# Solve steps uncut and split otherwise over the slots, two decays moved into the first solve's slots, a longer pause ahead of a solve, some conversion steps on VectorE, nine weight loads issued sooner

## The chip, the cores and the metric

The kernel runs on one core of a Trainium2 chip. The metric is the device time of one execution in microseconds (us), lower is better. The engines are TensorE (PE; its weight loads are listed apart as PEld), VectorE (DVE), ScalarE (ACT), GpSimd (POOL) and SyncE (SP), which issues the DMA transfers.

## What is computed

Three stages follow one another. The first is a recurrence over 768 time steps for 4 x 8 heads of width 40, the second a gated layer of three weight matrices over 3072 tokens, the third a layer with a softmax-weighted activation and a normalisation.

```python
for t in range(S):                       # S = 768
    y[:, :, t] = einsum('bhd,bhde->bhe', r_t, state)
    Sa = einsum('bhde,bhe->bhd', state, a_t)
    state = state * w_t[..., None, :] - einsum('bhd,bhe->bhde', Sa, b_t) + einsum('bhd,bhe->bhde', v_t, k_t)
x = y.transpose(0, 2, 1, 3).reshape(3072, 320)
x = (sigmoid(x @ w_gate) * (x @ w_val)) @ w_out          # 320 -> 1536 -> 320
h = x @ w_in                                             # 320 -> 1024
e = exp(h - max(h)); u = h * e / (sum(e) + 1e-9)
out = ((u - mean(u)) / sqrt(var(u) + 1e-6) * g_ln) @ w_out2
```

## The kernel before

**Recurrence.** Time is cut into 24 chunks of 32 steps, and the 32 heads into two sets, which gives 48 slots s = 0 to 47. Two chunks form a superstep. Inside a chunk the state's update is a triangular system, so for each of the 12 supersteps a 32 x 32 unit-triangular matrix per head and chunk is inverted on VectorE. This is a solve, n = 0 to 11. A solve has 31 steps j (`t_iter`, L247 to L263), and a step is a multiplication into `tmp` (L258) and an addition into `pT` (L262), both over m = j//2+1 column groups of k = 31-j elements. In the solves n = 0 and n = 2 the steps from j = 6 on are `cut`: each of the two operations is made in two halves, so a step has four instructions. A solve reads its coefficients from the tile `M`, which is loaded back from DRAM (`t_load`, `M<-ab`), after TensorE's products were stored there (`ab<-abn`). Its result goes through ACT into `TT` (L268), to DRAM, and back as `TB`.

**Lookahead and slots.** The preparation of chunk data runs LOOK = 10 slots ahead, so slots are counted from s = -10; `begin` does the first four of them as a prologue and the loop over `slot` starts at s = -6. Solve 0 takes slots -6 to -3, eight steps in each. Solve n > 0 takes the four slots s = 4n-5 to 4n-2; `SOLVE` (L34) says at which steps it is split among them (k = 0 to 3), with one entry for n = 1, one for n = 2 and one for all n from 3 on. A decay (`decay`, L145 to L162, five VectorE instructions) turns a superstep's weights `G` into the factors that scale the chunk data. A decay is named by superstep and head set. `begin` does those of superstep 0, then (1,0), (1,1) and (2,0), the last three behind the first load of `M`.

**How a slot orders its work.** A slot has ten pieces of TensorE work (state products, the update, `pY` at L387 and others). VectorE's solve steps, decays and a pause form the list `back` of (cost, function). After each piece, entries are taken from `back` until their costs reach the sum that is left divided by the pieces that are left. The pause is an entry of cost WAIT with no function, ahead of a solve's first step. Only the order in which instructions stand in an engine's stream depends on this.

```python
share, left = [], sum(x for x, _ in back) / (len(work) - p)
while back and (left > 0 or p == len(work) - 1):
    x, f = back.pop(0)
    share.append(f)
    left -= x
fill(s, share)
```

**Layers beside it.** `Between.fill` (L940 to L968) mixes in the second stage: up to s = 5 the conversion of its weights, later its matrix products for the tokens that are done. The weights come as 64-bit floats and are converted by `Convert.value` (L594 to L610) into 32-bit ones: two ACT operations (L591, L592), four on VectorE (L603 to L608) and two on `self.eng` (L609, L610), which is POOL. A matrix product in 32-bit accuracy is made from high and low parts (`mm320`, L823), which ACT (L539) and POOL or VectorE (L540) split off. Behind the slots, from about 680 us to 945 us, `Late.first` (L1065) makes the remaining tokens' second stage; its `jobs2` convert the third stage's weights `w_in` and `w_out2` in the three places `l_cv`, each filled by a load of three DMAs (L624, and L529 twice). `Late.second` is the third stage.

**Queues.** All DMAs are issued by SP in the program's order; an engine takes its own instructions in the order in which they stand.

Of the kernel before, what the change touches and what calls it, by code (L numbers as in the profile page):

```python
# [17 lines left out]
ALU = mybir.AluOpType  # L18
# [6 lines left out]
CH = 32  # L25
# [5 lines left out]
KEEP = LOOK + 2  # L31
TS = SS * CH
WCOLS = TS + 2
SOLVE = (0, 0, 13, 26, 31), (0, 0, 11, 21, 31), (0, 12, 24, 28, 31)  # L34
WAIT = 2.0
LOAD = 6
SUMS = 6, 8
NF = 5
# [18 lines left out]
def run(gen, n=None):  # L57

    if gen is not None:
        for f in itertools.islice(gen, n):  # L60
            f()
# [6 lines left out]
class Attention:  # L68
# [178 lines left out]
    def t_iter(self, n, j):  # L247

        nc = self.nc
        M, TT = self.M[n], self.pT.rearrange("p (j t) -> p j t", t=CH)  # L250
        k, m = CH - 1 - j, j // 2 + 1
        tmp = self.tmp[j % 2][:, 0:m * k].rearrange("p (c t) -> p c t", t=k)

        cut = m // 2 if m >= 4 and n in (0, 2) else 0
        parts = [r for r in (slice(0, cut), slice(cut, m)) if r.stop > r.start]

        def mult(r):
            nc.vector.tensor_tensor(out=tmp[:, r], in0=TT[:, r, j:j + 1].broadcast_to([128, r.stop - r.start, k]),  # L258
                                    in1=M[:, j:j + 1, j + 1:CH].broadcast_to([128, r.stop - r.start, k]), op=ALU.mult)

        def add(r):
            nc.vector.tensor_tensor(out=TT[:, r, j + 1:CH], in0=TT[:, r, j + 1:CH], in1=tmp[:, r], op=ALU.add)  # L262
        return [(0.155 + (r.stop - r.start) * k * 0.00104, lambda r=r, f=f: f(r)) for f in (mult, add) for r in parts]  # L263

    def t_store(self, n):
        self.M.pop(n)
# [140 lines left out]
    def begin(self, dummy):  # L407

        self.w_load(1, 0)
        for i in (0, 1):  # L410
            self.clear(i)
        for i in (0, 1):
            self.w_sums(0, i)
        dummy(BEGIN[0])
        for i in (0, 1):
            for f in self.decay(0, i):
                f()
            self.scaled(i)
            if i == 0:
                self.scaled(2)  # L420
                self.w_load(1, 1)
                self.le_load(2 * SS)
                self.w_sums(1, 0)
        self.scaled(3)
        self.le_load(2 * SS + 1)
        self.w_load(2, 0)
        for k, i in enumerate((0, 2, 1, 3)):
            if k == 2:
                self.eye()
            run(self.products(i))  # L430
            dummy(BEGIN[1 + k])
        self.t_load(0)
        self.w_sums(1, 1)
        for n, hs in ((1, 0), (1, 1), (2, 0)):
            for f in self.decay(n, hs):
                f()

    def slot(self, s, fill):
        pi = s + LOOK
        pj = pi - 1  # L440
        on, last = 0 <= s < NHS, 1 <= s <= NHS

        back = []

        n, k = divmod(s - (2 * SS + 1 - LOOK), 2 * SS)
        if 0 < n < NSS:
            if k == 0:
                back += [(WAIT, None)]
            steps = range(*SOLVE[min(n, 3) - 1][k:k + 2])
            back += [f for j in steps for f in self.t_iter(n, j)]  # L450
            if k == 2 * SS - 1:
                back += [(0.0, lambda: self.t_store(n))]
        if s in range(-6, -2):
            back += [f for j in range((s + 6) * 8, min((s + 7) * 8, CH - 1)) for f in self.t_iter(0, j)]
        m, hs = pi // (2 * SS) + 1, (pi % (2 * SS)) // 2
        if pi % 2 and (2, 0) < (m, hs) < (NSS, 0):
            self.w_load(m, hs)
        if pi + 1 < NHS:
            if pi > 2 * SS:
                self.le_load(pi + 1)  # L460
            m, hs = divmod(pi + 1, 2 * SS)
            if hs < 2 and (m, hs) > (2, 0):
                back += zip((0.5, 1.3, 0.4, 1.3), self.decay(m, hs))
        late = s == -1
        if pi < NHS and not late:
            self.scaled(pi)
        ruv = self.m_ruv(s - 1) if last else None
        prod = self.products(pj) if 2 * SS <= pj < NHS else None
        work = [
            lambda: on and (run(self.m_r(s)), self.m_st(s)),  # L470
            lambda: run(ruv, 4),
            lambda: run(ruv),
            lambda: on and self.m_u(s),
            lambda: run(prod, 4),
            lambda: (run(prod), late and self.scaled(pi)),
            lambda: last and run(self.m_y(s - 1)),
            lambda: on and self.m_state(s),
            lambda: (on and self.m_ut(s), 0 <= s + 1 < NHS and self.natural(s + 1), self.loads(s + 2)),
            lambda: None]
        for p, f in enumerate(work):  # L480
            f()
            if p == LOAD and pj % (2 * SS) == 2 * SS - 1 and 2 * SS < pj < NHS:
                self.t_load(pj // (2 * SS))
            if p == 4 and s % 2 and 3 < s < NHS - 1:
                self.t_fetch((s + 1) // 2)
            if p == SUMS[pi % 2]:
                m, hs = divmod(pi + 2, 2 * SS)
                if hs < 2 and (2, 0) < (m, hs) < (NSS, 0):
                    self.w_sums(m, hs)
# [7 lines that stand above are left out]
        if s == -3:  # L497
            self.t_store(0)
            self.t_fetch(0)
        if s in (1, 3):  # L500
            self.t_fetch((s + 1) // 2)
# [213 lines left out]
def mix(take, n, other):  # L715

    other = list(other)
    for i in range(n):
        for f in [take()] + [other.pop(0) for _ in range(-(-len(other) // (n - i)))]:
            if f is not None:  # L720
                f()
    for f in other:
        if f is not None:
            f()
# [24 lines left out]
class Conversions:  # L749
# [47 lines left out]
    def next(self):  # L797

        if not self.todo and not self.over():
            self.todo = self.begin()  # L800
        return self.todo.pop(0) if self.todo else None
# [64 lines left out]
class Between:  # L866
# [68 lines left out]
    def dummy(self, k):  # L935
        z = self.zero
        for _ in range(k):
            self.nc.tensor.matmul(self.gv, lhsT=z[:, 0:128], rhs=z, start=True, stop=True)

    def fill(self, s, other, flat):  # L940

        p = self.seen[s] = self.seen.get(s, -1) + 1
        if s < FILL:
            if s >= -1:
                self.dummy(2 if s >= 0 or p > 3 else 0)
            if s == -5 and p < 3:
                self.jobs.load()
            self.cv.eng = self.nc.gpsimd
            mix(self.jobs.next, STEPS[s] if s >= 0 else 2 if s == -1 and p < 7 else 0, other)
            if s == FILL - 1:  # L950
                if p == FIRST[0]:
                    self.jobs.to(99)
                    self.begin(flat.memory)
                    self.load(0)
                if p == FIRST[1]:
                    self.ready(0)
            return
        b, k = divmod(s - FILL, 4)
        if p in LAST.get(s - NHS, UNITS) and not self.step(b):
            self.dummy(IDLE)  # L960
        mix(self.jobs2.next if not self.jobs2.over() or self.jobs2.todo else lambda: next(flat.run, None), LATER[self.jobs2.over()][p], other)
        if k == 3 and b + 1 < NT // 256:
            if p == NEXT[0]:
                if b == 1:
                    self.jobs2.to(99)
                self.load(b + 1)
            if p == NEXT[1]:
                self.ready(b + 1)  # L968
# [15 lines left out]
class Late:  # L984
# [80 lines left out]
    def first(self, btw):  # L1065
        nc, acc, hid = self.nc, [x[:, 0:D] for x in (self.lt[:, 0], self.lt[:, 1], self.one, self.three)], self.hid
        nc.sync.dma_start(out=self.gain, in_=self.d["moe2_g_ln"].rearrange("(k p) -> p k", p=128))
        tiles = [range(N0 if b == 0 else NF, 12) for b in range(6)]
        units = [(b, f) for b in range(6) for f in tiles[b]]

# [440 lines left out]
```

## Time and profile before

| | us |
|---|---|
| median of 3 runs | 1159.73 (1158.47 to 1161.88) |
| profiled execution: its time | 1161.03 |
| profiled execution: its span | 1159.3 |
| PE busy | 1030.9 (89%) |
| DVE busy | 792.8 (68%) |
| ACT busy | 594.5 (51%) |
| POOL busy | 466.7 (40%) |
| PE's mean granted clock | 0.947 of full speed |

The profile page divides the span into 40 slices of 29 us. VectorE is at 8 to 9 tenths in the first seven slices and at 7 to 9 up to the seventeenth; PE starts at 4 to 8 tenths and is at 8 or 9 from the tenth slice on. Slot 0 begins at about 65 us, slot 47 at about 643 us, `Late.first` at about 680 us and `Late.second` at about 945 us.

### The profile page before, as it was taken

To read this page: it belongs to the slowest core of one execution; us is meant where nothing else is said; L and a number is where in the kernel's file an instruction comes from. 1 tells how busy PE (TensorE), PEld (TensorE's weight loads), DVE (VectorE), ACT (ScalarE), POOL (GpSimd) and SP (SyncE) were. 2 spreads that over 40 slices of the span, in tenths; PEclk is the share of its full clock that TensorE was granted. 3 is DMA by queue.
4 is the path that set the end of the run, shared out by engine and by line. 5 is a ranking of instruction groups with operands and counts; after the bars stand their busy time and mean duration, and the time that the engine had idled before them with its cause. 6 is when DMAs were issued, how large, how long until landed. Compare 5 with 4: busy or idle time off the path is not lost.

```text
span 1159.3 us, 31815 instructions
## 1 busy us (share of the span) xinstructions
PE 1030.9 (89%) x12710; PEld 879.1 (76%) x12710; DVE 792.8 (68%) x2085; ACT 594.5 (51%) x1511; POOL 466.7 (40%) x489
## 2 busy tenths in 40 slices
PE   4287788898999998999999989799999998999997
PEld 2244457777787887888888888688888876888897
DVE  9869899888978879788683235334443369767673
ACT  5245455766666566675666444324343344444542
POOL 7564534446556456464221112234433301322232
PEclk8578998999999999999999989899999999999999
DMA  7564564668666776666534234302211000000001
GB/s 183 140 149 116 140 154 114 143 180 197 169 155 158 192 189 156 156 161 167 129 111 126 68 110 125 105 28 89 85 57 34 1 1 6 19 23 18 18 23 38
DMA packets 179451, 122.62 MB, mean 106 GB/s; under 512 B 106016, under 2 KB 159264, under 8 KB 179296
## 3 DMA queue, kind: packets, MB, share of 16 engines
q1 hardware_dynamic: 179296, 120.52, 40.1%
q8 instruction: 102, 1.67, 0.6%
q14 instruction: 53, 0.43, 0.1%
HBM read 98.94 MB, written 21.53 MB: 104 GB/s over the span
## 4 chain that ended last, share of the span: by engine, by line
PE 50%; DVE 23%; DMA 10%; ACT 7%; issue 4%; SPq 4%; POOL 1%; DVEq 0%; ACTq 0%; POOLq 0%
PE hid L823 20%; DVE pT L262 5%; DVE tmp L258 4%; PE one L823 4%; DMA b_plain<-xT 3%; PE three L1194 2%; DMA M<-ab 2%; PE three L1197 2%; PE three L1195 2%; PE pY L387 2%; DVE RL L374 2%; PE pruv L370 2%; PE two L1181 2%; PE two L856 2%; PE two L858 2%
## 5 line engine op out<-in xcount | busy, mean ns | idle before, releaser
L823 PE MATMUL hid<-l_x,l_w 128*128 128x512 f32 x672 | 161.3, 392 | 0.0
L823 PEld LDWEIGHTS hid<-l_x,l_w 128*128 128x128 f32 x672 | 125.2, 189 | 24.4 <-issue 0.2
L823 PE MATMUL one<-b_tokens,b_w 128*128 128x256 f32 x816 | 128.8, 302 | 2.1 <-DVE b_plain L844 1.7
L258 DVE TENSOR_TENSOR tmp<-pT,M 128x30 f32<-128x30 f32 (+34 forms) x422 | 96.8, 239 | 41.7 <-DMA M<-ab 32.8
L224 POOL TENSOR_TENSOR AT<-abn,mA 64x256 f32<-64x256 f32 x96 | 81.8, 852 | 82.1 <-ACT abn L219 77.2
L823 PEld LDWEIGHTS one<-b_tokens,b_w 128*128 128x128 f32 x816 | 107.7, 197 | 7.8 <-DVE b_plain L844 1.9
L262 DVE TENSOR_TENSOR pT<-pT,tmp 128x30 f32<-128x30 f32 (+34 forms) x422 | 105.2, 249 | 12.3
L540 POOL TENSOR_TENSOR l_x<-l_plain,l_x 128x512 fp32r<-128x512 f32 x43 | 55.6, 1292 | 119.6 <-ACT l_x L539 100.5
L540 POOL TENSOR_TENSOR b_tokens<-b_plain,b_tokens 128x256 fp32r<-128x256 f32 x58 | 47.6, 820 | 125.4 <-ACT b_tokens L539 113.0
L823 PE MATMUL hid<-b_w,l_x 128*128 128x512 f32 x384 | 94.0, 397 | 2.6 <-DVE l_e L1153 2.6
L844 DVE TENSOR_TENSOR l_plain<-hid,l_plain 128x512 f32<-128x512 f32 x43 | 29.7, 691 | 95.1 <-ACT l_plain L843 95.1
L207 PE MATMUL pABK<-AT,BK 128*64 128x64 f32 x768 | 62.4, 239 | 34.9 <-POOL BK L197 33.9
L207 PEld LDWEIGHTS pABK<-AT,BK 128*64 128x64 f32 x768 | 54.5, 150 | 45.7 <-POOL BK L197 36.2
L823 PEld LDWEIGHTS hid<-b_w,l_x 128*128 128x128 f32 x384 | 70.9, 188 | 19.0 <-DVE l_e L1153 3.6
L196 POOL TENSOR_TENSOR AT<-AT,G 40x256 f32<-40x256 f32 x90 | 69.0, 766 | 33.4 <-DVE G L162 19.3
L387 PE MATMUL pY<-RL,YR 128*64 128x32 f32 (+1 forms) x1536 | 59.8, 220 | 24.8 <-DVE RL L374 21.8
L387 PEld LDWEIGHTS pY<-RL,YR 128*40 128x40 f32 (+1 forms) x1536 | 52.1, 131 | 37.3 <-DVE RL L374 22.0
L843 ACT ACTIVATE l_plain<-hid 128x512 f32<-128x512 f32 x43 | 25.6, 595 | 95.2 <-PE hid L823 95.2
L314 ACT ACTIVATE Z<-pu 32x160 f32<-32x160 f32 x192 | 56.2, 293 | 28.6 <-PE pu L311 25.5
L539 ACT ACTIVATE b_tokens<-b_plain 128x256 fp32r<-128x256 f32 (+1 forms) x70 | 33.9, 488 | 63.6 <-DVE b_plain L844 45.5
L370 PE MATMUL pruv<-RL,UV 128*64 128x64 f32 x768 | 58.9, 232 | 6.4 <-ACT YR L237 2.7
L1188 POOL TENSOR_TENSOR l_w<-l_e,l_w 128x1024 fp32r<-128x1024 f32 x12 | 28.8, 2400 | 88.7 <-ACT l_e L1149 51.1
(253 smaller groups left out, 2593.2 us busy)
## 6 DMA issues: line engine op xcount, KB each, us to landing
AT<-in_LA_dram SPq DMA_DIRECT2D x48, 256.0 KB
RL<-in_RS_dram SPq DMA_DIRECT2D x24, 512.0 KB
LB<-in_LB_dram SPq DMA_DIRECT2D x46, 208.0 KB
Z<-in_VN_dram SPq DMA_DIRECT2D x48, 160.0 KB
M<-ab SPq DMA_DIRECT2D x24, 256.0 KB
UV<-in_VT_dram SPq DMA_DIRECT2D x24, 208.0 KB
G<-in_LW_dram SPq DMA_DIRECT2D x22, 214.5 KB
xT<-yt SPq DMA_DIRECT2D x24, 160.0 KB
```

What stands on the lines that cost most here:

```text
L196: eng.tensor_tensor(out=at[SROW[g], g], in0=at[SROW[g], g], in1=G[SROW[g]], op=ALU.mult)
L207: yield lambda m=m: nc.tensor.matmul(ps[0:64, m * 64:m * 64 + 64], lhsT=bkt[:, m].rearrange("p s t -> p (s t)"), rhs=at[:, :, m, :], start ...
L224: nc.gpsimd.tensor_tensor(out=at[UROW[g], g].rearrange("p (a b) t -> p a b t", a=2), in0=abn[UROW[g], :, hs], in1=self.mA[UROW[g]].unsquee ...
L258: nc.vector.tensor_tensor(out=tmp[:, r], in0=TT[:, r, j:j + 1].broadcast_to([128, r.stop - r.start, k]), in1=M[:, j:j + 1, j + 1:CH].broad ...
L262: nc.vector.tensor_tensor(out=TT[:, r, j + 1:CH], in0=TT[:, r, j + 1:CH], in1=tmp[:, r], op=ALU.add)
L314: nc.scalar.activation(z[32 * q:32 * q + 32, hs, g, p * 4:p * 4 + 4, :], ps[32 * q:32 * q + 32, 0:160].rearrange("p (h d) -> p h d", d=40) ...
L370: yield lambda p=p, hh=hh, m=m: nc.tensor.matmul(ps[0:64, m * 64:m * 64 + 64], lhsT=uvt[:, hs * 4 + hh, 64 * p:64 * p + 64], rhs=rl[:, hs, ...
L387: yield lambda m=m, g=g, at=at: nc.tensor.matmul(ps[rows[g], m * CH:m * CH + CH], lhsT=flat[:, at:at + rows[g].stop - rows[g].start], rhs= ...
L539: nc.scalar.activation(h, src, AF.Copy)
L540: eng_l.tensor_tensor(out=l, in0=src, in1=h.bitcast(F32), op=ALU.subtract)
L823: nc.tensor.matmul(out, lhsT=a, rhs=b, start=n == 0, stop=n == 7)
L844: self.nc.vector.tensor_tensor(out=self.sg, in0=self.pv, in1=self.sg, op=ALU.mult)
```

## The change

SOLVE's entry for n from 3 on goes from 12, 12, 4 and 3 steps in the four slots to 9, 12, 6 and 4. WAIT goes from 2 to 4. No step is cut any more. The decays (1,1) and (2,0) leave `begin` and come into the slots -6 and -3. L609 and L610 go to VectorE while s < 3. `Late.first` issues the loads of all three `l_cv` places right behind the load of the gain.

```diff
@@ -31,8 +31,8 @@
 KEEP = LOOK + 2
 TS = SS * CH
 WCOLS = TS + 2
-SOLVE = (0, 0, 13, 26, 31), (0, 0, 11, 21, 31), (0, 12, 24, 28, 31)
-WAIT = 2.0
+SOLVE = (0, 0, 13, 26, 31), (0, 0, 11, 21, 31), (0, 9, 21, 27, 31)
+WAIT = 4.0
 LOAD = 6
 SUMS = 6, 8
 NF = 5
@@ -251,16 +251,12 @@
         k, m = CH - 1 - j, j // 2 + 1
         tmp = self.tmp[j % 2][:, 0:m * k].rearrange("p (c t) -> p c t", t=k)
 
-        cut = m // 2 if m >= 4 and n in (0, 2) else 0
-        parts = [r for r in (slice(0, cut), slice(cut, m)) if r.stop > r.start]
-
-        def mult(r):
-            nc.vector.tensor_tensor(out=tmp[:, r], in0=TT[:, r, j:j + 1].broadcast_to([128, r.stop - r.start, k]),
-                                    in1=M[:, j:j + 1, j + 1:CH].broadcast_to([128, r.stop - r.start, k]), op=ALU.mult)
-
-        def add(r):
-            nc.vector.tensor_tensor(out=TT[:, r, j + 1:CH], in0=TT[:, r, j + 1:CH], in1=tmp[:, r], op=ALU.add)
-        return [(0.155 + (r.stop - r.start) * k * 0.00104, lambda r=r, f=f: f(r)) for f in (mult, add) for r in parts]
+        def mult():
+            nc.vector.tensor_tensor(out=tmp, in0=TT[:, 0:m, j:j + 1].broadcast_to([128, m, k]), in1=M[:, j:j + 1, j + 1:CH].broadcast_to([128, m, k]), op=ALU.mult)
+
+        def add():
+            nc.vector.tensor_tensor(out=TT[:, 0:m, j + 1:CH], in0=TT[:, 0:m, j + 1:CH], in1=tmp, op=ALU.add)
+        return [(0.155 + m * k * 0.00104, f) for f in (mult, add)]
 
     def t_store(self, n):
         self.M.pop(n)
@@ -431,9 +427,8 @@
             dummy(BEGIN[1 + k])
         self.t_load(0)
         self.w_sums(1, 1)
-        for n, hs in ((1, 0), (1, 1), (2, 0)):
-            for f in self.decay(n, hs):
-                f()
+        for f in self.decay(1, 0):
+            f()
 
     def slot(self, s, fill):
         pi = s + LOOK
@@ -459,7 +454,7 @@
             if pi > 2 * SS:
                 self.le_load(pi + 1)
             m, hs = divmod(pi + 1, 2 * SS)
-            if hs < 2 and (m, hs) > (2, 0):
+            if hs < 2 and (m, hs) > (1, 0):
                 back += zip((0.5, 1.3, 0.4, 1.3), self.decay(m, hs))
         late = s == -1
         if pi < NHS and not late:
@@ -945,7 +940,7 @@
                 self.dummy(2 if s >= 0 or p > 3 else 0)
             if s == -5 and p < 3:
                 self.jobs.load()
-            self.cv.eng = self.nc.gpsimd
+            self.cv.eng = self.nc.vector if s < 3 else self.nc.gpsimd
             mix(self.jobs.next, STEPS[s] if s >= 0 else 2 if s == -1 and p < 7 else 0, other)
             if s == FILL - 1:
                 if p == FIRST[0]:
@@ -1065,6 +1060,8 @@
     def first(self, btw):
         nc, acc, hid = self.nc, [x[:, 0:D] for x in (self.lt[:, 0], self.lt[:, 1], self.one, self.three)], self.hid
         nc.sync.dma_start(out=self.gain, in_=self.d["moe2_g_ln"].rearrange("(k p) -> p k", p=128))
+        for _ in self.jobs2.cv.raw:
+            self.jobs2.load()
         tiles = [range(N0 if b == 0 else NF, 12) for b in range(6)]
         units = [(b, f) for b in range(6) for f in tiles[b]]
```

VectorE's order at the end of the prologue, before: the two decays `G1_1` and `G2_0`, then step 0 of solve 0 (`M0`).

```order
L145 TENSOR_SCALAR G1_1_270<-G1_1_270 104x8x64
L155 SCALAR_TENSOR_TENSOR Q0_189<-G1_1_270,d1_150 104x528
L159 RECIPROCAL d1_150<-Q0_189 104x8
L160 COPY PE1_1_376<-Q0_189 104x8
L162 SCALAR_TENSOR_TENSOR G1_1_270<-G1_1_270,d1_150 104x528
L145 TENSOR_SCALAR G2_0_292<-G2_0_292 104x8x64
L155 SCALAR_TENSOR_TENSOR Q1_190<-G2_0_292,d1_150 104x528
L159 RECIPROCAL d1_150<-Q1_190 104x8
L160 COPY PE2_0_382<-Q1_190 104x8
L162 SCALAR_TENSOR_TENSOR G2_0_292<-G2_0_292,d1_150 104x528
L258 TENSOR_TENSOR tmp0_187<-pT_185,M0_365 128x31
L262 TENSOR_TENSOR pT_185<-pT_185,tmp0_187 128x31
```

VectorE's order with the change, at the end of solve 0's first eight steps (lines of the functions behind `t_iter` are three to five lower).

```order
L255 TENSOR_TENSOR tmp0_187<-pT_185,M0_365 128x100
L258 TENSOR_TENSOR pT_185<-pT_185,tmp0_187 128x4x25
L255 TENSOR_TENSOR tmp1_188<-pT_185,M0_365 128x96
L258 TENSOR_TENSOR pT_185<-pT_185,tmp1_188 128x4x24
L145 TENSOR_SCALAR G1_1_270<-G1_1_270 104x8x64
L155 SCALAR_TENSOR_TENSOR Q0_189<-G1_1_270,d1_150 104x528
L159 RECIPROCAL d1_150<-Q0_189 104x8
L160 COPY PE1_1_376<-Q0_189 104x8
L162 SCALAR_TENSOR_TENSOR G1_1_270<-G1_1_270,d1_150 104x528
L255 TENSOR_TENSOR tmp0_187<-pT_185,M0_365 128x115
L258 TENSOR_TENSOR pT_185<-pT_185,tmp0_187 128x5x23
```

Decay (1,1) now stands inside solve 0, between its eighth and ninth step; decay (2,0) stands behind solve 0's last step, ahead of decay (2,1).

VectorE's order at the first steps of solve 6 (`M6`) before; RL is the mask over the state's read rows that `pY` needs, `b_plain` a split of the second stage.

```order
L608 TENSOR_SCALAR flat_135<-flat_135 128x224
L258 TENSOR_TENSOR tmp0_187<-pT_185,M6_4730 128x31
L262 TENSOR_TENSOR pT_185<-pT_185,tmp0_187 128x31
L258 TENSOR_TENSOR tmp1_188<-pT_185,M6_4730 128x30
L262 TENSOR_TENSOR pT_185<-pT_185,tmp1_188 128x30
L374 TENSOR_TENSOR RL1_182<-pruv18_4841,mR_148 64x256 x2
L844 TENSOR_TENSOR b_plain_126<-one_123,b_plain_126 128x256
```

The same place with the change.

```order
L603 TENSOR_SCALAR flat_135<-flat_135 128x224
L255 TENSOR_TENSOR tmp0_187<-pT_185,M6_4630 128x31
L258 TENSOR_TENSOR pT_185<-pT_185,tmp0_187 128x31
L255 TENSOR_TENSOR tmp1_188<-pT_185,M6_4630 128x30
L370 TENSOR_TENSOR RL1_182<-pruv18_4741,mR_148 64x256 x2
L839 TENSOR_TENSOR b_plain_126<-one_123,b_plain_126 128x256
L258 TENSOR_TENSOR pT_185<-pT_185,tmp1_188 128x30
```

Three solve instructions instead of four stand ahead of RL; the first step stands where it stood.

SP's order at the start of `Late.first`, before.

```order
L656 DMA l_plain<-late_moe_w_out 128x320
L1067 DMA b_plain<-in_moe_g_ln_dram 128x8x1
L925 DMA x2d_116<-b_plain 128x2x320
L862 DMA l_plain<-xT_66 128x2x256
L529 DMA l_plain<-xT_66 64x256 x2
```

The same place with the change.

```order
L651 DMA l_plain<-late_moe_w_out 128x320
L1062 DMA b_plain<-in_moe_g_ln_dram 128x8x1
L619 DMA l_cv<-in_moe_w_in_dram 128x2x256
L524 DMA l_cv<-in_moe_w_in_dram 64x256 x2
L619 DMA l_cv<-in_moe_w_in_dram 128x2x256
L524 DMA l_cv<-in_moe_w_in_dram 64x256 x2
L619 DMA l_cv<-in_moe_w_in_dram 128x2x256
L524 DMA l_cv<-in_moe_w_in_dram 64x256 x2
L920 DMA x2d_116<-b_plain 128x2x320
```

The nine DMAs, which stood behind the loads for the second block of tokens, now stand ahead of the store of the last `x2d` block and of all that follows.

## Rows read from the trace of the kernel before

**Rows 1.** The page's chain that ended last: shares of the span by engine.

```profile
PE 50%; DVE 23%; DMA 10%; ACT 7%; issue 4%; SPq 4%; POOL 1%; DVEq 0%; ACTq 0%; POOLq 0%
```

**Rows 2.** Windows: stretch, length, busy us (PE, PEld, DVE, ACT, POOL), clock, DMA share, GB/s.

```profile
65.00:132.00 67.00, 49.57 (x718) 28.85 (x705) 50.28 (x133) 36.37 (x106) 36.32 (x40) 0.90 0.65 158
132.00:196.00 64.00, 51.25 (x848) 37.26 (x850) 59.88 (x199) 32.19 (x96) 29.46 (x36) 0.87 0.51 127
```

**Rows 3.** VectorE's timeline, prologue and solve 0: start, duration, instruction, [idle before <-releaser].

```profile
21.35 0.68 DVE L145 TENSOR_SCALAR G<-G 104x512 f32<-104x512 f32 x1
...
29.57 0.19 DVE L258 TENSOR_TENSOR tmp<-pT,M 128x31 f32<-128x31 f32 x1
...
38.89 0.35 DVE L258 TENSOR_TENSOR tmp<-pT,M 128x54 f32<-128x54 f32 x2
...
39.81 0.36 DVE L258 TENSOR_TENSOR tmp<-pT,M 128x68 f32<-128x68 f32 x2
```

**Rows 4.** ACT's timeline: `TT` copy behind solve 0, a gate weight, the late `l_cv`.

```profile
54.31 0.60 ACT L268 ACTIVATE TT<-pT 128x512 f32<-128x512 f32 x1 [10.48 <-DVE pT L262]
...
75.21 0.55 ACT L591 ACTIVATE b_raw<-b_raw 128x384 f32<-128x384 f32 x1 [6.56 <-DMA b_raw<-in_moe_w_gate_dram]
...
745.89 0.55 ACT L591 ACTIVATE l_cv<-l_cv 128x384 f32<-128x384 f32 x1 [11.26 <-DMA l_cv<-in_moe_w_in_dram]
```

**Rows 5.** SP's timeline: loads of `M` for solve 0, a gate weight, the first `l_cv`.

```profile
24.78 1.16 SPq L529 DMA_DIRECT2D M<-ab  x2
...
68.75 0.39 SPq L624 DMA_DIRECT2D b_raw<-in_moe_w_gate_dram  x1
...
740.95 0.47 SPq L624 DMA_DIRECT2D l_cv<-in_moe_w_in_dram  x1
```

**Rows 6.** VectorE's timeline, slots 0 to 5.

```profile
70.92 0.19 DVE L258 TENSOR_TENSOR tmp<-pT,M 128x31 f32<-128x31 f32 x1 [6.51 <-DMA M<-ab]
...
87.46 0.28 DVE L258 TENSOR_TENSOR tmp<-pT,M 128x126 f32<-128x126 f32 x1
...
88.11 0.30 DVE L258 TENSOR_TENSOR tmp<-pT,M 128x136 f32<-128x136 f32 x1
...
105.09 1.19 DVE L608 TENSOR_SCALAR b_plain<-b_plain 128x320 int32<-128x320 int32 x1
...
120.18 0.48 DVE L563 TENSOR_TENSOR b_w<-b_raw,b_w 128x320 fp32r<-128x320 f32 x1
...
121.76 0.36 DVE L608 TENSOR_SCALAR b_plain<-b_plain 128x384 int32<-128x384 int32 x1
...
130.28 0.42 DVE L554 TENSOR_TENSOR b_w<-b_raw,b_w 128x256 fp32r<-128x256 f32 x1 [3.83 <-ACT b_w L552]
```

**Rows 7.** POOL's timeline: a conversion operation that changes engine.

```profile
106.36 0.86 POOL L609 TENSOR_TENSOR b_plain<-b_plain 128x320 f32<-128x320 f32 x1 [0.26 <-DVE b_plain L608]
```

**Rows 8.** Waits ahead of all solve multiplications (L258): releaser, us, times; then solve 6's first.

```profile
  DMA M<-ab: 32.8, 9
...
330.34 0.19 DVE L258 TENSOR_TENSOR tmp<-pT,M 128x31 f32<-128x31 f32 x1 [4.75 <-DMA M<-ab]
```

**Rows 9.** The page's costliest groups: busy us, mean ns | idle before, releaser.

```profile
L387 PE MATMUL pY<-RL,YR 128*64 128x32 f32 (+1 forms) x1536 | 59.8, 220 | 24.8 <-DVE RL L374 21.8
```

**Rows 10.** PE's timeline: `pY` in the second slots of solves 4 and 11, first and last of seven.

```profile
249.81 1.46 PE L387 MATMUL pY<-RL,YR 128*64 128x32 f32 x32 [0.75 <-DVE RL L374]
...
583.73 1.36 PE L387 MATMUL pY<-RL,YR 128*64 128x32 f32 x32 [0.65 <-DVE RL L374]
```

**Rows 11.** PE's timeline in `Late.first`: twelve products and the group of 16 behind them, twice.

```profile
750.19 0.63 PE L856 MATMUL two<-l_w,l_x 128*128 128x320 f32 x1 [8.21 <-ACT l_x L539]
...
754.37 4.80 PE L823 MATMUL hid<-l_x,l_w 128*128 128x512 f32 x16
...
759.01 0.30 PE L856 MATMUL two<-l_w,l_x 128*128 128x320 f32 x1
...
760.77 3.81 PE L823 MATMUL hid<-l_x,l_w 128*128 128x512 f32 x16
```

## The prediction

> **What bounds the kernel now.** I read the chain that ended last first [rows 1]: half of the span is TensorE, but 23% is VectorE and 10% DMA, so the kernel has stretches with different limits, and each edit has to be priced in its own. The windows come next [rows 2]. In slots 0 to 5 VectorE is busy 50.28 of 67 us, then 59.88 of 64, while TensorE has 49.57 and 51.25: there VectorE sets the pace, and what it is given or spared moves the end. Then come the timelines of VectorE and ACT around solve 0. Its first step is at 29.57 [rows 3], and ACT waited 10.48 us until 54.31 for its result [rows 4]: the solve is on the path. From solve 4 on VectorE has spare time: it waits for the load of `M` for 32.8 us in nine places [rows 8], the 6.51 of solve 1 among them [rows 6]. There TensorE is the bound, and what of VectorE's work costs time shows as TensorE's wait for the mask RL, 21.8 us over the whole program [rows 9]. Behind the slots TensorE is alone on the path, with one visible hole: 8.21 us ahead of 750.19 [rows 11].
>
> **Solve 0 uncut, decay (1,1) inside it.** A cut step j = 13 lasts from 38.89 to 39.81, 0.92 us [rows 3]; the same step of solve 1, which is uncut, from 87.46 to 88.11, 0.65 us [rows 6]. The difference of 0.27 over the 25 steps from j = 6 on is 6.75; the steps differ a little in size, and I take 6.5. Against it stands the decay. Two decays take from 21.35 to 29.57, 4.1 us each [rows 3], and solve 0 follows without an idle. They seem to be on the path ahead of the solve, but the load of `M` that the solve needs is issued only at 24.78 and takes SP 1.16 us [rows 5], and solve 1 waited for such a load [rows 6], so I take it that the load lands at about 29 and that the decays ran under its cover. Moved into the solve, decay (1,1) has no cover. I price it at 3.8, a bit under 4.1, since less runs beside it there; its bounds are 0, if the load lands early enough for the solve to start sooner by as much, and 4.1. Decay (2,0) falls behind the solve's last step, while the solve's result is on its way through DRAM, and costs nothing there; without that cover it costs 4.1 as well. Net: -6.5 + 3.8 = **-2.7** (bounds -6.5 and +1.7).
>
> **Conversions on VectorE.** Fourteen operations L609 and L610 go from POOL to VectorE. The nearest VectorE operation with two inputs and 320 columns lasted 0.48 [rows 6], so I take 0.5 each. Four of them stand ahead of slot 0's VectorE-bound stretch, under waits like the 6.51; ten stand in it: +5.0. What is given back: POOL took 0.86 for one [rows 7], so each pair is done some 0.7 us sooner, and VectorE's operations behind it wait less; the 3.83 at 130.28 is a wait of that chain [rows 6]. I take half the cost, -2.5, hence about **+2.3** with the small steps rounded (bounds -2.5, all cover, and +7.0, fourteen and no relief).
>
> **Solve 2 uncut.** The same 25 steps, in the window in which VectorE is busy 59.88 of 64 us [rows 2]: **-6.5** (bounds 0, if ACT or the loads set the pace, and -6.75).
>
> **Other split of solves 3 to 11, and the pause.** The order shows the pause to be without effect: the entry is taken first and alone whatever its cost, and the first step stands where it stood. I price it at nothing; a first step that still waits 2 to 5 us for `M` is its check. The split takes three steps of about 0.65 out of the first slot, 1.95 us per solve, at most 17.6 over nine solves. They matter only where TensorE waits because of them. Its waits for RL in the second slots, into which the first slot's steps run over, are seven, from 0.75 to 0.65, in all 5.8 us [rows 10]. I take **-5.5** (bounds 0 and -17.6): the row that measures the overrun, not the one that measures the work. What is late next is the load of `M`.
>
> **Late loads.** The first `l_cv` load is issued at 740.95 [rows 5]; ACT, which takes its work in order, waits 11.26 for it at 745.89 [rows 4], the splits of TensorE's operand stand behind it, and TensorE stands still for 8.21 [rows 11]. After the hole TensorE ran slower: twelve products took 750.19 to 754.37, 4.18 us, against 759.01 to 760.77, 1.76, and the group behind them 4.80 against 3.81 [rows 11]. So 8.21 + 2.42 + 0.99 = 11.6. With the loads issued at the start of `Late.first`, at about 680 and so some 60 us sooner, nothing of the wait is left: **-11.5** (bounds -8.2, if the slower products come from something else, and -11.6, before the price). The price: SP's issue of one place's three DMAs takes 0.47 and some 1.16 us [rows 5], so 4.9 for three places, ahead of the `x2d` store and the next loads of tokens and weights. I take these to be issued well ahead of their use, so that none of it reaches TensorE; if all of it did, -6.6 would be left.
>
> **Sum.** -2.7 + 2.3 - 6.5 - 5.5 - 11.5 = -23.9. The profiled execution took 1161.03 (its span is 1159.3), so it would take **1137.1**; it lies 1.3 us above the median of 1159.73, which is within the spread of the runs, and I forecast 1137.
>
> **The rivals.** *Only the late loads count* (0.15). The first slots may be paced by transfers and ACT: VectorE's 3.83 is a wait for ACT [rows 6], and ACT's gate weight came 6.56 late, its load issued at 68.75 [rows 4, 5]. Then an earlier end of the solves is spent in these waits. Against it: the windows, in which VectorE has under 5 us free in 64. It gives 1161.0 - 11.5 = 1149.5.
>
> *The moved conversions cost more than their price* (0.12). VectorE's mask L608 took 1.19 beside POOL's work and 0.36 without it, on more columns [rows 6]. If each of the ten moved operations is stretched by the difference, 0.83, that is +8.3: 1145.4. Against it: taking the pair from POOL also takes POOL's work from beside VectorE. The Trainium skill ("SBUF — State Buffer", section "Who interferes with whom") has a rule that speaks for it: a VectorE instruction with two inputs in SBUF contends with a GpSimd instruction that reads SBUF, and the later of the two waits for the whole of the other. By that rule the moved operations, which have two inputs, would meet POOL's neighbours; L608 has one input and was stretched too, so the trace does not settle which operations are hit.
>
> *The split or the pause cures the waits for `M` too* (0.06). If half of the 26.3 us of waits behind solve 1 [rows 6, 8] leaves TensorE's path, some 10 more are gained: 1127. The order speaks against it.
>
> *Slower: the steps only move to where they hurt* (0.05). The third and fourth slots of each solve get three steps more, 1.95 us, and if TensorE waits for RL behind them and half of the loss of 2.42 after a hole [rows 11] comes with it, that is 3.15 per solve, 28.4 over nine. With the -5.5 gone: 1161.0 - 18.4 + 28.4 = 1171. It decides from 18.4/9 = 2.05 us per solve on. Against it: TensorE's waits for RL that I read lie nearly all in the first and second slots, so the later two have room.
>
> **How the numbers follow.** The forecast has 0.62. A change under 0.3%, 3.5 us, could not be told from none. The forecast and the first three rivals are faster, all but a part of the first where the late loads give less as well; of the last a sliver is no change: faster 0.94, same 0.02, slower 0.04. The range reaches from 1128, the forecast with the split at two thirds of its bound and the decay free, to 1150, which takes in the first two rivals; it leaves out the third and the last, and the forecast's edges.
>
> **What would show it.** ACT's copy of `TT` behind solve 0 at about 51.5 instead of 54.31. A step j = 13 of 0.65 in solves 0 and 2. POOL without L604 and L605 ahead of slot 3, and VectorE's rows of them near 0.5. TensorE without a hole at 750 less the gain so far, and no slow products behind it. The first steps of solves 4 to 11 still waiting for `M`, and RL's 21.8 down by about 5. The forecast is wrong if slots 0 to 5 do not become shorter by some 7 us, or if the late hole only moves to another load.

## The result and the profile after

The changed kernel takes 1141.13 us in the median (1140.12 to 1142.68, four runs) against 1159.96 of the kernel before in the same measurement: a ratio of 0.9838, 95% interval 0.9819 to 0.9857, so 18.8 us less. A second measurement, `after2`, gave 1140.86 against 1160.45, ratio 0.983 (0.9808 to 0.9853). Below I take the mean of the two ratios, 0.9834 or 19.3 us, as the level of the changed kernel, and turn ratios into time with 1160 us, so 0.001 is 1.16 us. The difference of two such ratios is uncertain by some 4 us.

The profiled execution took 1140.12, with a span of 1138.3; the one of before had 1159.3. I start again with the chain that ended last, which is to be held against [rows 1].

```profile
PE 53%; DVE 22%; DMA 11%; ACT 5%; SPq 4%; issue 3%; POOL 1%; DVEq 0%; ACTq 0%; POOLq 0%
```

TensorE's share went up and ScalarE's down; VectorE's is hardly less. To see where the 21 us between the two spans lie, I used the 48 masks RL on VectorE, one per slot, as marks. The mask of a chunk stands one slot later than the chunk's own, so the first mark lies in slot 1. The first is 3.2 us earlier than before, the sixth 5.2, the ninth 8.4, and the last six 10.3. So **in this execution 10.3 us come from the slots and 10.7 from what lies behind them.** One caution: the profiled execution of `after2`, 1145.31, is only 6.6 us ahead of before in the last slot. A single trace places a gain to some 4 us; the medians say how large it is.

Around solve 0, VectorE's timeline of the changed kernel (start, duration, instruction, [idle before <-releaser]):

```profile
29.67 0.19 DVE L255 TENSOR_TENSOR tmp<-pT,M 128x31 f32<-128x31 f32 x1 [8.37 <-DMA M<-ab]
...
33.79 0.42 DVE L145 TENSOR_SCALAR G<-G 104x512 f32<-104x512 f32 x1
...
37.02 0.25 DVE L255 TENSOR_TENSOR tmp<-pT,M 128x115 f32<-128x115 f32 x1
...
40.21 0.29 DVE L255 TENSOR_TENSOR tmp<-pT,M 128x126 f32<-128x126 f32 x1
...
40.87 0.30 DVE L255 TENSOR_TENSOR tmp<-pT,M 128x136 f32<-128x136 f32 x1
```

With the decays gone VectorE stands still for 8.37 us and the solve begins at the same moment as in [rows 3]: the load of `M` had been the cover. Decay (1,1) then takes 33.79 to 37.02, 3.23 us, inside the solve. An uncut step j = 13 takes 0.66 in place of 0.92. ScalarE's copy of the result shows the sum; it stood at 54.31 in [rows 4].

```profile
50.86 0.60 ACT L264 ACTIVATE TT<-pT 128x512 f32<-128x512 f32 x1 [1.57 <-DVE pT L258]
```

The same two windows in the changed kernel, to be held against [rows 2]. They reach to the end of slot 7, and not only of slot 5: TensorE begins slot 8 at 195.8 us before. VectorE's load in the first window rose from 50.28 to 57.32 us, GpSimd's fell from 36.32 to 24.70, and TensorE makes 59 and 118 more of its products in the same time.

```profile
65.00:132.00 67.00, 51.98 (x777) 31.03 (x776) 57.32 (x150) 37.56 (x109) 24.70 (x27) 0.86 0.63 155
132.00:196.00 64.00, 56.00 (x966) 42.75 (x967) 58.67 (x164) 36.77 (x109) 34.14 (x38) 0.91 0.50 122
```

In the slots of solves 3 to 11 three views answer to [rows 8] and [rows 9]. The waits ahead of all solve multiplications (releaser, us, times):

```profile
  DMA M<-ab: 29.9, 8
```

VectorE's timeline at solve 6's first step, with the mask RL behind it:

```profile
324.78 0.19 DVE L255 TENSOR_TENSOR tmp<-pT,M 128x31 f32<-128x31 f32 x1 [4.02 <-DMA M<-ab]
...
325.46 0.87 DVE L370 TENSOR_TENSOR RL<-pruv,mR 64x256 f32<-64x256 f32 x2
```

The page's group of `pY` (busy us, mean ns | idle before, releaser):

```profile
L383 PE MATMUL pY<-RL,YR 128*64 128x32 f32 (+1 forms) x1536 | 58.0, 219 | 21.0 <-DVE RL L370 16.4
```

The waits for `M` are still there: 8.37 of the 29.9 is solve 0's, which leaves 21.5 in seven places against 26.3 in eight before, and the eighth, solve 11's, is a wait of 3.77 us for ScalarE here. RL's 21.8 became 16.4. The waits of the second slots, 5.8 us in [rows 10], are gone altogether; those of the first slots, 6.5 us, stayed.

In the late part SP's first `l_cv` load, ScalarE's first work on it, and TensorE's stretch of 80 us in which the hole of [rows 11] had been:

```profile
673.60 0.57 SPq L619 DMA_DIRECT2D l_cv<-in_moe_w_in_dram  x1
```

```profile
725.51 0.53 ACT L586 ACTIVATE l_cv<-l_cv 128x384 f32<-128x384 f32 x1
```

```profile
680.00:760.00 80.00, 80.00 (x415) 70.28 (x414) 37.65 (x66) 34.46 (x72) 25.58 (x21) 1.00 0.29 85
```

Before, this window read as follows.

```profile
680.00:760.00 80.00, 71.34 (x358) 62.27 (x357) 32.21 (x54) 29.72 (x62) 19.71 (x17) 0.93 0.36 103
```

The twelve slow products behind the hole [rows 11] lay, before, in this stretch:

```profile
750.20:754.30 4.10, 3.65 (x12) 3.25 (x13) 3.49 (x5) 1.97 (x4) 2.62 (x2) 0.50 0.19 60
```

TensorE had stood still for 8.21 us, and its granted clock was then 0.50, the lower of its two levels (1.2 GHz). A product took 0.47 us there and 0.31 from 759 us on, at a clock of 1.00. One of the twelve also waited 0.45 us for GpSimd, so the clock's part of the prediction's 2.42 is some 2.0. In the changed kernel ScalarE's 11.26 us of waiting for `l_cv` are gone, TensorE is busy all 80 us, and its granted clock is 1.00 in place of 0.93. A smaller wait ahead of this stretch grew: TensorE's wait for ScalarE's split `b_tokens` was 2.91 us, until 675.20, and is 5.22, until 666.34. That mark is only 8.9 us earlier, so 1.4 of the 10.3 were given back there. From it to the end the changed kernel is 12.1 us shorter.

### The profile page after: what moved, and what is told of

It is laid out like the page before. It is cut to its first block, busy times and chain, and to the rows that moved or that the text cites. A ratio compares the mean times of both kernels' runs of the same rounds, so it can differ in the third digit from the quotient of the medians.

```text
span 1138.3 us, 31716 instructions
## 1 busy us (share of the span) xinstructions
PE 1024.5 (90%) x12710; PEld 875.4 (77%) x12710; DVE 782.9 (69%) x1999; ACT 594.5 (52%) x1511; POOL 451.6 (40%) x475
## 4 chain that ended last, share of the span: by engine, by line
PE 53%; DVE 22%; DMA 11%; ACT 5%; SPq 4%; issue 3%; POOL 1%; DVEq 0%; ACTq 0%; POOLq 0%
PE hid L818 21%; DVE pT L258 4%; DVE tmp L255 4%; PE one L818 4%; DMA M<-ab 3%; PE three L1191 2%; PE three L1194 2%; PE three L1192 2%; PE pruv L366 2%; DVE RL L370 2%; PE two L851 2%; DMA b_plain<-xT 2%; PE two L853 2%; PE two L1178 2%; PE pY L383 2%
## 5 line engine op out<-in xcount | busy, mean ns | idle before, releaser
L255 DVE TENSOR_TENSOR tmp<-pT,M 128x126 f32<-128x126 f32 (+22 forms) x372 | 93.1, 250 | 42.0 <-DMA M<-ab 29.9
L224 POOL TENSOR_TENSOR AT<-abn,mA 64x256 f32<-64x256 f32 x96 | 78.3, 815 | 98.9 <-ACT abn L219 94.3
L258 DVE TENSOR_TENSOR pT<-pT,tmp 128x126 f32<-128x126 f32 (+22 forms) x372 | 96.7, 260 | 10.7
L535 POOL TENSOR_TENSOR b_tokens<-b_plain,b_tokens 128x256 fp32r<-128x256 f32 x58 | 50.8, 876 | 119.5 <-ACT b_tokens L534 111.5
L818 PEld LDWEIGHTS hid<-b_w,l_x 128*128 128x128 f32 x384 | 72.1, 191 | 19.3 <-DVE l_e L1150 3.6
L383 PE MATMUL pY<-RL,YR 128*64 128x32 f32 (+1 forms) x1536 | 58.0, 219 | 21.0 <-DVE RL L370 16.4
L383 PEld LDWEIGHTS pY<-RL,YR 128*64 128x64 f32 (+1 forms) x1536 | 51.2, 130 | 32.4 <-DVE RL L370 14.6
L933 PE MATMUL one<-zero 128*128 128x512 bf16 x196 | 63.3, 431 | 1.8 <-DVE lim L96 1.3
```

What stands on the lines that cost most here:

```text
L224: nc.gpsimd.tensor_tensor(out=at[UROW[g], g].rearrange("p (a b) t -> p a b t", a=2), in0=abn[UROW[g], :, hs], in1=self.mA[UROW[g]].unsquee ...
L255: nc.vector.tensor_tensor(out=tmp, in0=TT[:, 0:m, j:j + 1].broadcast_to([128, m, k]), in1=M[:, j:j + 1, j + 1:CH].broadcast_to([128, m, k] ...
L258: nc.vector.tensor_tensor(out=TT[:, 0:m, j + 1:CH], in0=TT[:, 0:m, j + 1:CH], in1=tmp, op=ALU.add)
L383: yield lambda m=m, g=g, at=at: nc.tensor.matmul(ps[rows[g], m * CH:m * CH + CH], lhsT=flat[:, at:at + rows[g].stop - rows[g].start], rhs= ...
L535: eng_l.tensor_tensor(out=l, in0=src, in1=h.bitcast(F32), op=ALU.subtract)
L818: nc.tensor.matmul(out, lhsT=a, rhs=b, start=n == 0, stop=n == 7)
```

## The experiments

**The decays back in the prologue.** `u_decay`, from the changed kernel:

```diff
-        for f in self.decay(1, 0):
-            f()
+        for n, hs in ((1, 0), (1, 1), (2, 0)):
+            for f in self.decay(n, hs):
+                f()
...
-            if hs < 2 and (m, hs) > (1, 0):
+            if hs < 2 and (m, hs) > (2, 0):
```

> The changed kernel with the decays (1,1) and (2,0) back in the prologue. Theory (the prediction's): in the changed kernel VectorE stands idle for 8.37 us ahead of solve 0, waiting for M, and decay (1,1) then takes 3.2 us inside the solve; put back, both decays are hidden under that wait, solve 0 ends about 3.2 us sooner, and the kernel takes about 1138 us. Rival: solve 0's end does not set slots 0 to 5 any more (the products that go through GpSimd, their store and the load of M for solve 1 do), and the time stays at 1141, or gets longer because the early slots' VectorE work is moved.

Measured: 1139.07 us, ratio to the kernel before 0.9802 (0.9781 to 0.9822). Against the level of 0.9834 that is 3.7 us less. ScalarE's copy behind solve 0 in its trace:

```profile
48.68 0.60 ACT L264 ACTIVATE TT<-pT 128x512 f32<-128x512 f32 x1 [2.96 <-DVE pT L258]
```

In this execution the solve began at 30.60, so from first step to copy it took 18.1 us against 21.2 in the changed kernel: the decay's 3.1. The place and the price of the decay are shown. That all of it reaches the end is what the median says, within an uncertainty as large as the effect. The rival is not excluded: solve 1's first step waits for `M` again, as it did before the change.

```profile
65.75 0.19 DVE L255 TENSOR_TENSOR tmp<-pT,M 128x31 f32<-128x31 f32 x1 [5.80 <-DMA M<-ab]
```

In the changed kernel this step stands at 67.87 and waits for no load, since VectorE is at work without a wait from solve 0 on. So 2.1 us are gained up to here in these two traces, and what sets the time here is the load.

**The conversions on GpSimd again.** `u_conv`, and the same kernel once more as `u_conv2`:

```diff
-            self.cv.eng = self.nc.vector if s < 3 else self.nc.gpsimd
+            self.cv.eng = self.nc.gpsimd
```

> The changed kernel with all of the last two conversion operations on GpSimd again. Theory (the prediction's): VectorE is spared ten operations of 0.5 us in the stretch that it bounds, less half of that for longer waits behind GpSimd; the kernel gets faster by 2.3 us, to about 1139, and slots 0 to 3 gain about that. Rival: GpSimd's own queue (the scalings at L196 and L197 that the products wait for) is the bound there, and the kernel gets slower, to about 1144.

> The changed kernel with the last two conversion operations on GpSimd again, a second time and on another chip, since the first gave a ratio to the kernel before of 0.977 against 0.983 to 0.984 of the changed kernel, three times the 2.3 us that the prediction charged. Theory A (the prediction's price): a ratio of 0.981 to 0.982. Theory B (the moved operations are stretched beside GpSimd, and VectorE's queue is long there): 0.976 to 0.978 again.

Measured: 1135.57 us, 0.9773 (0.9752 to 0.9793), and 1141.04 us, 0.9814 (0.9786 to 0.9843). The first says 7.1 us, the second 2.3, which is theory A's range, but its interval takes in theory B's 0.978 and no effect too. The second run did not come to another chip: both are on record for chip 6. The sign is that of the prediction: VectorE should not have been given this work. The size stays open between the two. What the moved operations last is in VectorE's timeline of the changed kernel, here two of the first six and one of the eight behind them.

```profile
65.63 0.85 DVE L604 TENSOR_TENSOR b_plain<-b_plain 128x384 f32<-128x384 f32 x1
66.52 1.43 DVE L605 TENSOR_TENSOR b_raw<-b_plain 128x384 f32<-128x384 f32 x1
...
83.49 0.56 DVE L604 TENSOR_TENSOR b_plain<-b_plain 128x384 f32<-128x384 f32 x1
```

GpSimd's timeline beside the first two:

```profile
64.31 1.75 POOL L196 TENSOR_TENSOR AT<-AT,G 40x256 f32<-40x256 f32 x2
66.15 1.39 POOL L197 TENSOR_TENSOR BK<-LB,Q 104x512 f32<-104x512 f32 x1
```

Three of the fourteen lasted 0.80 to 1.43 us, and all three began while GpSimd was in such an instruction; the first two end 0.42 and 0.41 us behind the end of the GpSimd instruction that was running when they began. Ten others, which have none beside them for longer than 0.05 us, lasted 0.54 to 0.56 with 384 columns and 0.48 and 0.49 with 320. The trace agrees here with the rule of the Trainium skill that the prediction named ("SBUF — State Buffer", section "Who interferes with whom"), but the move itself takes away most of the GpSimd work that could stretch them. The rival of 0.83 us on each of ten is excluded as to its size by this trace: of the ten operations behind the first four only one reached 0.80, and their sum is 5.6 us; over all fourteen the stretching comes to some 1.5 us.

The prediction put four of the fourteen at nothing, under the wait of 6.51 ahead of solve 1, and decay (2,0) under the way of solve 0's result through DRAM. In the changed kernel both stand in the same gap: the decay 3.2 us, the four operations 3.4, two of them stretched. They fill it, and solve 1's first step, at 67.87 (68.15 in `after2`), waits for no load. With the conversions back on GpSimd it comes at 66.56 and 66.49, behind waits for `M` of 1.29 and 1.74. So what was priced at nothing delays solve 1 by 1.3 to 1.7 us.

**Solve 2 cut again, and both solves cut again.** `u_cut2` and `u_cuts` put back

```diff
+        cut = m // 2 if m >= 4 and n in (2,) else 0
+        parts = [r for r in (slice(0, cut), slice(cut, m)) if r.stop > r.start]
```

with the two operations made for each part; `u_cuts` has `n in (0, 2)`.

> The changed kernel with the steps of solve 2 cut in halves again. Theory (the prediction's): solve 2 lies in a stretch that VectorE bounds, so 25 steps at 0.26 us more cost 6.5 us, and the kernel takes about 1147.6. Rival: from the traces the slots of solve 2 became only 2.2 to 3.4 us shorter, so that ScalarE or loads set the pace behind it, and the kernel takes 1143 to 1144.5.

> The changed kernel with the steps of both solves 0 and 2 cut in halves again. The prediction's price of the cuts is 13 us, ratio to the kernel before 0.994 to 0.995. Rival: solve 0 passes on its 6.5 us, and solve 2 only some 2 us, since the later slots wait less for M when it is late and give the rest back: 7 to 9 us, ratio 0.990.

Measured: `u_cut2` 1144.49 us, 0.9848 (0.9823 to 0.9873), 1.6 us over the changed kernel's level; `u_cuts` 1151.9 us, 0.9902 (0.9874 to 0.993), 7.9 us over it. In the traces, solve 2 from its first step to the copy of its result lasts 39.8 us before, 34.6 in the changed kernel, and 39.7 when cut again. So 5 us were saved inside solve 2, and what came through at the end is nearer to 1.6, with an interval of some 3.4 us to either side that leaves out the forecast's 6.5. In `u_cut2` TensorE waited for RL 13.3 us in all, against 16.4 and 18.1 in the two traces of the changed kernel: later slots took part of the delay up.

```profile
L387 PE MATMUL pY<-RL,YR 128*64 128x32 f32 (+1 forms) x1536 | 57.2, 219 | 14.8 <-DVE RL L374 13.3
```

The marks show where. The first three of `u_cut2` agree with those of `after2` within 0.2 us; then it is 3.2 us behind at the sixth mark, 4.6 at the ninth, 4.8 at the fourteenth, 2.2 at the seventeenth and 1.8 at the last. Most of what is given back lies in the slots of solve 5, where VectorE's wait for `M` is 1.03 us instead of 2.68 and TensorE's wait of 1.88 for RL is gone. Against the first trace of the changed kernel the delay grows by 6.1 us up to the eighth mark and ends at 2.8. Solve 0, by the difference of the two runs, passes on about 6.3 us; from its first step to the copy it lasts 27.8 us when cut and 21.2 when not.

**The old split of solves 3 to 11.** `u_split`:

```diff
-SOLVE = (0, 0, 13, 26, 31), (0, 0, 11, 21, 31), (0, 9, 21, 27, 31)
+SOLVE = (0, 0, 13, 26, 31), (0, 0, 11, 21, 31), (0, 12, 24, 28, 31)
```

> The changed kernel with the old split of the solves 3 to 11 (12, 12, 4 and 3 steps). Theory (the prediction's): the new split is worth 5.5 us, nearly all in the second slots; the kernel takes about 1146.6, and the second slots of the solves become longer by about 14 us together, the third and fourth shorter by about 9. Rival: these gains were carried over from the solves 0 and 2, and the split moves nothing: 1141.

Measured: 1143.47 us, 0.9841 (0.982 to 0.9863), 0.8 us over the level of the changed kernel, with no clear sign. The traces are clearer. From RL mark to RL mark over the 36 slots of solves 3 to 11, second slots take 111.6 us before, 97.3 in the changed kernel and 112.1 with the old split; third and fourth slots together 185.9, 195.0 and 185.6; all four kinds 427.4, 422.3 (421.8 in its second trace) and 425.5. TensorE's waits for RL with the old split are back in the second slots, 5.9 us in six of them, the largest 1.44. The other runs' traces bear it out: with the old split (before, `u_split`, `only_late`) the second slots take 111.6 to 112.2 us and the 36 slots 425.5 to 427.9; with the new split and the pause of the change, in eight traces, 97.1 to 99.2 and 418.4 to 428.0, in the mean 422.4.

So the split does what the prediction said where it said, and is worth 3 to 5 us in these slots, 4.5 by the means; two thirds of what the second slots gain go to the third and fourth.

**The late loads alone.** `only_late`, from the kernel before (and the changed kernel once more beside it, `after2`):

```diff
         nc.sync.dma_start(out=self.gain, in_=self.d["moe2_g_ln"].rearrange("(k p) -> p k", p=128))
+        for _ in self.jobs2.cv.raw:
+            self.jobs2.load()
```

> The changed kernel again, on the chip of the three runs beside it. Expected of every theory: the ratio to the kernel before stays at 0.984, within its interval; it is the measure for what single parts are worth, since the level differs between chips by up to 2 us.

> The kernel before with the nine late loads alone issued sooner. Theory (the prediction's): the hole of 8.21 us and the slow products behind it go, 11.5 us, ratio to the kernel before 0.990. Rival: the loads delay the last tokens' loads and the x2d store, which lie behind them on SynchE's queue, and some of the hole opens elsewhere: 5 to 8 us, ratio 0.993 to 0.996.

Measured: `after2` as told above; `only_late` 1150.77 us, 0.991 (0.9883 to 0.9937), 10.4 us less than the kernel before (7.3 to 13.6). The forecast of 11.5 stands, and the hole at 750 us is absent from its trace. From the last mark to the end the kernel before takes 508.2 us, and the thirteen traces with the late loads 493.3 to 499.0, which is 9.2 to 14.9 less. The price that the prediction feared, nine loads ahead of others, does not show: the wait for `b_tokens` that grew to 5.22 in the changed kernel is 2.43 here, so the loads alone do not cause it.

**A pause that acts.** The cost 4 in one entry gives the same order as the cost 2: either way the entry takes up the share of the slot's first piece of work and nothing more. So I made the entry into eight:

```diff
-                back += [(WAIT, None)]
+                back += [(WAIT / 8, None)] * 8
```

> The changed kernel with a pause that acts: eight entries of 0.5 in place of one of 4.0, so that a solve's first step comes behind the mask RL in its first slot and VectorE does not wait for M ahead of RL. Theory (the rival of the prediction that the pause cures the waits): VectorE's wait for M, 26 us in eight places, falls to a few us, TensorE's waits for RL in the first slots (5.7 us) go, and the kernel gets 3 to 6 us faster than the changed one. Rival: the first slot's nine steps are crowded into its second half and overrun into the second slot, where TensorE waits for RL instead; the time stays or gets longer by up to 5 us.

Measured: 1132.48 us, 0.9758 (0.9735 to 0.978), against 0.983 of `after2`, measured beside it: 8.4 us less, more than expected. VectorE's timeline in the first slot of solve 6:

```profile
321.87 0.87 DVE L370 TENSOR_TENSOR RL<-pruv,mR 64x256 f32<-64x256 f32 x2
...
325.56 0.19 DVE L255 TENSOR_TENSOR tmp<-pT,M 128x31 f32<-128x31 f32 x1 [0.17 <-DMA M<-ab]
```

The waits ahead of all solve multiplications:

```profile
  DMA M<-ab: 12.6, 6
```

RL now stands ahead of the first step, and behind solve 0 (9.23 of the 12.6) only 3.4 us of waits for `M` are left of 21.5. The page's group of `pY`:

```profile
L383 PE MATMUL pY<-RL,YR 128*64 128x32 f32 (+1 forms) x1536 | 56.5, 218 | 12.3 <-DVE RL L370 9.9
```

By the RL marks the 36 slots take 413.1 us against 422.3; first slots 103.0 against 130.0 (RL itself comes sooner in them), second slots 117.7 against 97.3, so the overrun of the rival is there too but is smaller than the gain. In the two traces of the next experiment that have this pause the 36 slots take 414.0 and 415.4 us, in the eight without it 418.4 to 428.0.

**The pause with the losses of the change undone.** `pause_conv` has the conversions on GpSimd, `pause_both` also the decays in the prologue (diffs as above). `u_both`, the same without the acting pause, ran beside `after2`.

> The changed kernel with the decays back in the prologue and all conversion operations on GpSimd. Theory (now): each of the two is a loss inside the change, the decay because it lost the cover of M's load (3.2 us at solve 0), the conversions because VectorE bounds slots 0 to 5 (5 us of work and its stretching beside GpSimd); together the kernel is 5 to 10 us faster than the changed one, ratio to the kernel before 0.975 to 0.979. Rival: both gain on the same path, so that undoing both gives no more than undoing the conversions alone (a ratio of 0.977 in the earlier runs), or the gain of that run was the chip's.

> The changed kernel with the pause that acts (eight entries of 0.5) and with all of the last two conversion operations on GpSimd. Theory: the pause gains in the slots of solves 3 to 11, the conversions in slots 0 to 5, so the gains add: with 8 us from the pause and 2 to 7 from the conversions, a ratio to the kernel before of 0.970 to 0.974. Rival: what the first slots gain is given back by the waits for M behind them, and the ratio stays at the 0.976 of the pause alone.

> As the kernel beside it, and with the decays (1,1) and (2,0) back in the prologue under the wait for M, where they cost nothing; solve 0 ends 3.2 us sooner. Theory: 3 us more than the kernel beside it, ratio 0.967 to 0.972. Rival: solve 1's own chain (the products, their store and the load of M) takes the 3 us up, and the two agree within 1 us.

Measured: `u_both` 1139.32 us, 0.9805 (0.978 to 0.983), 2.9 us under `after2`, outside the range expected and less than the two single runs together, though their uncertainty is as large as the difference; `pause_conv` 1131.05 us, 0.9737 (0.9707 to 0.9766); `pause_both` 1131.05 us, 0.9722 (0.9696 to 0.9748). Against the pause alone these are 2.4 and 4.2 us less, both within the uncertainty; the acting pause is what counts. The two agree within 1.7 us, so neither the 3 us expected of the decays nor the rival of under 1 us is excluded. `pause_both` is the best ratio of all: 32 us under the kernel before and 13 under the changed one. One reason why the two losses do not add shows at solve 1: in `u_both` its first step stands at 66.21, behind a wait of 5.95 us for `M`, no sooner than at 65.75 with the decays alone back. Undoing either one already brings the step to where the load sets the time.

## Why the prediction was right

The forecast was 1137 in a range of 1128 to 1150, by a sum of -23.9; measured were 1141 and -19.3. One term, solve 2, was over-valued by about as much as the 4.6 us between them (6.5 against 1.6). But the terms do not close the sum: with 2.3 for the conversions and -6.3 + 3.7 = -2.6 for solve 0, the medians of the single runs add up to -2.6 + 2.3 - 1.6 - 0.8 - 10.4 = -13.1, or to -16.8 if the split is given the 4.5 of its traces. Each is uncertain by some 3 to 4 us, and a part that is undone alone is partly taken up by waits behind it. So the forecast is right in its largest terms, and that the total came out so near is in part luck. By its steps:

- **Solve 0 (-2.7).** Right, in its parts too: the load of `M` was the cover, the solve starts at the same time, the decay costs 3.2 where 3.8 was taken, and the copy comes 3.45 us sooner. Cut again, solve 0 costs about 6.3 at the end for 6.5 forecast, and the decay undone gives 3.7. Decay (2,0), put at nothing, is not free: with the conversions it fills the gap ahead of solve 1.
- **Conversions (+2.3).** Right in sign; the two measurements, 2.3 and 7.1, do not settle the size. The prediction's own working gives +2.5. Four of the operations were not covered by solve 1's wait as it took them to be, since decay (2,0) used the same wait.
- **Solve 2 (-6.5).** This is the term that was mis-sized. Inside the solve 5 us were saved, but the end moved by 1.6. The prediction took the window in which VectorE is busy 59.88 of 64 us as if a gain there were kept to the end; the slots behind it take up half of it or more, where VectorE waits for `M` and TensorE for RL.
- **Split (-5.5) and pause (0).** Right in the slots: the waits in the second slots went from 5.8 to nothing, and the 36 slots became 5.1 to 5.6 us shorter, 4.5 by the means of eleven traces. The median of `u_split` shows less, 0.8, within its uncertainty. The longer pause changes nothing in the order, as said; the waits for `M` behind solve 1 are still 21.5 us, of 26.3.
- **Late loads (-11.5).** Right: 10.4 alone. The clock's part of it is borne out: 0.50 behind the hole before, and 1.00 over the window of 80 us now.

Of the prediction's signs, the copy of `TT`, the step of 0.65, the absent hole, the first steps still waiting for `M` and RL's 21.8 less 5 came out as said; GpSimd has none of the moved operations ahead of slot 3, and eleven of the fourteen on VectorE lasted near 0.5. The sign for being wrong, slots 0 to 5 not shorter by some 7 us, is left undecided: the seventh mark, the last inside the windows of [rows 2], comes 6.6 us sooner in the first trace and 2.4 in the second, the eighth 8.7 and 4.6.

Of the rivals, "only the late loads count" would have given 1149.5 and fell, since the slots gained too. The stretched conversions fell as to their size in the trace, though the 7.1 us of one run are near the 8.3 of that rival. The slower case fell: third and fourth slots did become 9 us longer, but over all four the split gains. The third rival, that the waits for `M` can be cured, did not happen here only because the pause of the change does not act: made to act, it is worth 8.4 us, near the 10 that the rival named.

## What to carry to other kernels

Before you price a scheduling constant, look whether the order of instructions changes with it: a cost in one list entry that is taken first and whole delays by one piece of work, however large it is. An instruction that waits for a DMA should stand behind the work on its engine that others wait for; moving the solves' first steps behind a mask was worth 8.4 us, about as much as all the edits of the recurrence in this change together. And work that seems to stand on the path ahead of a load-bound step may lie under the load: moved away, it costs its time: 3.2 us inside solve 0. And a wait can cover work only once: the second decay and four conversion operations were both counted under the one ahead of solve 1.

## What was not expected

Two profiled executions of one program, 1140.12 and 1145.31, differ by 3.7 us in the slots alone, with the same instructions in the same order; a gain of 3 us in a stretch of such a kernel can't be read from one trace of each.

The gains do not seem to add: decays and conversions undone gave 3.7 and 2.3 to 7.1 us singly but 2.9 together, and 5 us saved in one solve left 1.6 at the end. The traces show part of what takes these up, the loads of `M` for solve 1 and for the solves from 4 on and the waits for RL. How much of the 19.3 us belongs to each edit stays open.
